# Weight loads and gathers that wait for one-element stores, and five operations of a token sort that run on VectorE

## The chip, the cores and the metric

One core of a Trainium2 chip runs the whole kernel. The metric is device time in microseconds (us) of one execution; each kernel is executed several times and the median counts. TensorE (PE) multiplies matrices, VectorE (DVE), ScalarE (ACT) and GpSimd (POOL) work on tiles, SyncE (SP) issues most of the DMAs, and POOL issues the indirect ones, the gathers and scatters by a list of row numbers.

## The reference

Three stages on 3072 tokens (4 sequences of 768) of width 384, all in float32:

```python
y = attn(r, k, v, w, u)            # linear attention with a decaying state, 8 heads of 48
e = argmax(x @ w_gate); g = softmax(x @ w_gate)[e]          # x: y, a row for each token
o = sigmoid(x @ w_output_gate)[e]
x = g * o * (relu(x @ w1[e]) @ w2[e])                       # one of 8 experts, 384 -> 1024 -> 384
out = (silu(x @ w_gate2) * (x @ w_val2)) @ w_out2           # 384 -> 1536 -> 384
```

## The kernel before

Each float32 product is made of three matmuls of rounded parts (high and low), so every weight and every activation is first split: ACT casts the high part, DVE subtracts it to get the low part.

**Order.** The attention stage, up to some 130 us, stands in an order written out by hand. The expert stage (130 to 370 us) and the last stage (370 us to the end) are put in order, engine by engine, by a scheduler when the program is built. On the chip each engine then runs its own list in that order, and an instruction waits for semaphores of the others. SP's list is one queue of DMA issues: an issue that waits holds up every later one.

**The expert stage.** Experts are taken by falling count of tokens, as positions e = 0 to 7, each with room for `CAPS[e]` tokens (416 to 360). For each position `run` goes through eight steps f, a step being 128 of the 1024 hidden columns: `step` multiplies w1 into PSUM (`ph`, two buffers), ACT and DVE make `h` out of it (L1207, L1208), and `second` multiplies w2 into `py` two steps later. Position 0 is done in two parts: its first 256 tokens inside the attention stage's pools (`head`, tiles `pha` and `pya`), the other 160 in `run`. So `run` begins with eight short steps (lines 1184 and 1185), and position 1 follows.

**Weights.** A group is two steps' worth of one expert: `r1` for w1 and `r2` for w2, 384 KB each, which `load` fetches into one of four raw buffers. Groups 0 to 3 are position 0's, 4 to 7 position 1's. `prefetch` splits a group (L1060 on ACT, L1063 on DVE) three groups ahead of its use, and then the raw buffer takes the group four further on. Before the first step, `run` issues groups 4 to 7 in one go.

**Tokens.** `gather` fetches a position's tokens by up to four indirect DMAs of 128 rows into `xg` (POOL, L1140), and `transposed` turns them on PE (`pt`, L1154) and splits them into `x` (L966, L967). There are two sets of these tiles, for even and for odd positions. The code asks for position e + 1 at step f = 3 of position e; the scheduler may put it earlier.

**Beside it**, `widen` turns the last stage's weights into float32 in 36 pieces, each with four DVE operations (L1025 to L1034) and one on POOL (L1031), and `sorted_positions` finds where each token goes, a few operations at a time between the steps: among them `t0` (L726), `dsel` (L741) and the four products of `dsel` (L744, L749; on DVE L746) with 576 elements in each partition.

Of the kernel before, what the change touches and what calls it, by code (L numbers as in the profile page):

```python
# [15 lines left out]
ALU = mybir.AluOpType  # L16
# [4 lines left out]
P = 128  # L21
# [7 lines left out]
CAPS = (416, 416, 412, 404, 392, 384, 372, 360)  # L29
# [9 lines left out]
def moe_kernel(ctx, tc, cst, small, tok, tr, u, w1, w2, m_gate, m_val, m_out, out):  # L39
    nc = tc.nc  # L40
    NT, DM = out.shape
# [3 lines left out]
    NTILE = NT // P  # L45
# [7 lines left out]
    NJ = -(-CAP // P)  # L53
# [12 lines left out]
    ident, mask, niota, rev8, slot, tile_i, part_i, lead, caps = (  # L66
        cs[:, at[n]] for n in ("ident", "mask", "niota", "rev", "slot", "tile", "part", "lead", "caps")
    )
# [9 lines left out]
    rows = const.tile([P, E * NJ], I32, name="rows")  # L78
# [196 lines left out]
    def ins(t, n, at):  # L275
        if at == 1:
            return t.rearrange("p (o e) -> p o e", o=1).to_broadcast([P, n, t.shape[1]])
        return t.rearrange("p (e o) -> p e o", o=1).to_broadcast([P, t.shape[1], n])
# [407 lines left out]
    def sorted_positions(pool, pool_ps):  # L686
# [36 lines left out]


        t0 = pool.tile([P, NTILE, E], F32, name="t0", bufs=1)
        nc.gpsimd.tensor_tensor(out=t0, in0=oh_all, in1=ins(off_f, NTILE, 1), op=ALU.mult)  # L726
        yield
        dpf = pool.tile([P, NTILE], F32, name="dpf")
        nc.vector.reduce_sum(dpf, t0, axis=AX.X)
# [11 lines left out]
        nc.vector.tensor_tensor(out=dsel, in0=ins(dhif, NTILE, 2), in1=ins(tile_i, NTILE, 1), op=ALU.is_equal)  # L741
        dsel2 = pool.tile([P, NTILE, 5, NTILE], BF16, name="dsel2", bufs=1)
        yield
        nc.gpsimd.tensor_tensor(out=dsel2[:, :, 0, :], in0=dsel, in1=ins(tile_i, NTILE, 2), op=ALU.mult)  # L744
        yield
        nc.vector.tensor_scalar(out=dsel2[:, :, 1, :], in0=dsel, scalar1=part_i, scalar2=None, op0=ALU.mult)  # L746
        for j in range(3):
            yield
            nc.gpsimd.tensor_tensor(out=dsel2[:, :, 2 + j, :], in0=dsel, in1=ins(scale3[:, j, :], NTILE, 2), op=ALU.mult)  # L749
        psd = pool_ps.tile([P, 5, NTILE], F32, name="psd", tag="pd")  # L750
        for i in range(0, NTILE, 4):
            doh = pool.tile([P, 4, P], BF16, name="doh", bufs=1)
# [218 lines left out]
class MoE:  # L971
# [67 lines left out]
                yield  # L1039
        nc.sync.dma_start(out=env["m32"][n - 1], in_=store)  # L1040

    def load(self, e, g):
        nc, env, GF = self.nc, self.env, 2
        if e and g == 0:
            self.ids[e] = bass.ds(nc.sync.value_load(env["ids"][0:1, e : e + 1], min_val=0, max_val=env["E"] - 1), 1)
        pe = self.ids[e]
        r1 = self.raw.tile([P, env["KD"], GF * P], F32, name="r1")
        nc.sync.dma_start(
            out=r1, in_=self.w1v[pe, :, :, g * GF * P : (g + 1) * GF * P].rearrange("o p k f -> (o p) k f")
        )  # L1050
        r2 = self.raw.tile([P, GF, env["DM"]], F32, name="r2")
        nc.sync.dma_start(out=r2, in_=self.w2v[pe, :, g * GF : (g + 1) * GF, :].rearrange("o p f d -> (o p) f d"))
        self.raws[e, g] = r1, r2

# [10 lines left out]
    def run(self, sorted_positions, gates, ffn):  # L1065
        nc, tc, env = self.nc, self.tc, self.env
        ident, x_d, rows, offs, yd = (env[x] for x in ("ident", "x_d", "rows", "offs", "yd"))
        CAP, NJ, KD, KF, DM, E, NT = (env[x] for x in ("CAP", "NJ", "KD", "KF", "DM", "E", "NT"))
        GF = 2
        c = self.c  # L1070
        early = ExitStack()
        self.cv = early.enter_context(tc.tile_pool(name="cv", bufs=2, reuse_waits="tile", side="right"))
        sp = early.enter_context(tc.tile_pool(name="sp", bufs=1, reuse_waits="tile", side="right"))
        self.xp.append(c.enter_context(tc.tile_pool(name="xp1", bufs=1, reuse_waits="tile")))
        p_y = c.enter_context(tc.tile_pool(name="p_y", bufs=1, space=PSUM, reuse_waits="tile"))
        p_h = c.enter_context(tc.tile_pool(name="p_h", bufs=2, space=PSUM, reuse_waits="tile"))
        p_t = c.enter_context(tc.tile_pool(name="p_t", bufs=2, space=PSUM, reuse_waits="tile"))
        p_d = c.enter_context(tc.tile_pool(name="p_d", bufs=1, space=PSUM, reuse_waits="tile"))

        NG = KF // GF  # L1080
        for n in range(len(PREFETCH), len(PREFETCH) + NG):
            self.load(*divmod(n, NG))

        def load_x(e, tiles):
            self.gather(e, tiles, rows[:, e * NJ + tiles[0] : (e + 1) * NJ], NT)
            return self.transposed(e, tiles, p_t, "pt")

        for _ in gates(sp):
            pass
        pos = sorted_positions(sp, p_d)  # L1090
        next(pos)
        for e in range(E):
            x, _ = self.xs.pop(e)
            sl = slice(0 if e else HEAD, CAPS[e])
            py = [p_y.tile([P, CAP], F32, name=f"py{d}") for d in range(KD)]
            for f in range(KF):
                if f % GF == 0:
                    wt = self.ahead.pop((e, f // GF))
                ph = p_h.tile([P, CAP], F32, name="ph")

                a, b = self.step(e, f, wt, x, sl, ph, py)
                with tc.issue_after(a), tc.issue_after(b):
                    if e == E - 1 and f == X_AT - 1:

                        nc.scalar.activation(ffn.warm, ffn.warm, AF.Sigmoid)
                    if e == E - 1 and X_AT <= f < X_AT + KD:
                        ffn.x_part(0, f - X_AT)
                    n = (e * KF + f) // GF + DIST
                    if len(PREFETCH) <= n < E * NG:
                        self.prefetch(*divmod(n, NG), f % GF)  # L1110
                        if f % GF == 1 and n + NG < E * NG:
                            self.load(*divmod(n + NG, NG))
                    if e * KF + f >= POS0 and f % POSK == 0:
                        next(pos, None)
                    if e * KF + f >= FILL0:
                        self.filler(FILLN)
                if (e, f) == (E - 1, 0):
                    for _ in pos:
                        pass
                    self.filler(1000)  # L1120
                    early.close()
                    self.first.close()
                    ffn.prepare()
                if f == 3 and e + 1 < E:
                    load_x(e + 1, range(-(-CAPS[e + 1] // P)))
        while self.pend:
            self.second()

    def gather(self, e, tiles, rows, last):

        nc, env = self.nc, self.env
        CAP, KD, DM = (env[x] for x in ("CAP", "KD", "DM"))
        pool = self.xp[e % 2]
        if tiles[0] == 0:
            x = pool.tile([P, 2, KD, CAP], F32R, name="x")
            self.xs[e] = x, pool.tile([P, env["NJ"], DM], F32, name="xg")
        xg = self.xs[e][1]
        for i, j in enumerate(tiles):
            n = min(P, CAPS[e] - j * P)
            nc.gpsimd.indirect_dma_start(  # L1140
                out=xg[0:n, j, :], out_offset=None, in_=env["x_d"][0:last, :],
                in_offset=bass.IndirectOffsetOnAxis(ap=rows[0:n, i : i + 1].bitcast(U32), axis=0),
            )
# [357 lines left out]
```

## Time and profile before

| what | value |
|---|---|
| median of 3 runs | 820.11 us (818.72 to 823.32) |
| the profiled execution | 828.89 us |
| its span, from the first to the last instruction | 827.1 us |
| mean granted clock of TensorE in it | 0.991 |
| PE busy | 790.2 us, 96% of the span |
| DVE, ACT, POOL busy | 515.1, 347.6, 210.6 us |

The profiled execution is one run with the hardware profiler on. Its rows are in us from the span's start. A row names the engine, the line of the kernel, the tiles written and read, and in brackets how long the engine had been idle before it and which instruction's end released it ("issue" where the profile shows nothing that it waited for). [...]

### The profile page before, as it was taken

To read this page: it belongs to the slowest core of one execution; us is meant where nothing else is said; L and a number is where in the kernel's file an instruction comes from. 1 tells how busy PE (TensorE), PEld (TensorE's weight loads), DVE (VectorE), ACT (ScalarE), POOL (GpSimd) and SP (SyncE) were. 2 spreads that over 40 slices of the span, in tenths; PEclk is the share of its full clock that TensorE was granted. 3 is DMA by queue.
4 is the path that set the end of the run, shared out by engine and by line. 5 is a ranking of instruction groups with operands and counts; after the bars stand their busy time and mean duration, and the time that the engine had idled before them with its cause. 6 is when DMAs were issued, how large, how long until landed. Compare 5 with 4: busy or idle time off the path is not lost.

```text
span 827.1 us, 15617 instructions
## 1 busy us (share of the span) xinstructions
PE 790.2 (96%) x5982; PEld 718.5 (87%) x5983; DVE 515.1 (62%) x1091; ACT 347.6 (42%) x791; POOL 210.6 (25%) x207
## 2 busy tenths in 40 slices
PE   7989779699999999999999999999999999999997
PEld 4877678688999999998888888888888888889997
DVE  7789997399999999955554335333533443344443
ACT  5878663364575576554432222212222222122322
POOL 6999951354524422200001000200020020001000
PEclk9999999899999999999999999999999999999999
DMA  8899933686777877342210000000000010001000
GB/s 322 297 361 334 332 128 108 215 268 194 253 222 260 252 245 253 89 139 86 86 59 32 19 1 13 39 0 1 14 39 1 0 45 1 1 7 40 1 20 24
DMA packets 61860, 99.28 MB, mean 120 GB/s; under 512 B 5461, under 2 KB 48105, under 8 KB 61776
## 3 DMA queue, kind: packets, MB, share of 16 engines
q1 hardware_dynamic: 58320, 88.34, 32.3%
q0 software_dynamic: 3456, 9.85, 3.5%
q8 instruction: 49, 0.80, 0.4%
q14 instruction: 35, 0.29, 0.1%
HBM read 81.64 MB, written 16.53 MB: 119 GB/s over the span
## 4 chain that ended last, share of the span: by engine, by line
issue 58%; PE 16%; DVE 4%; POOL 3%; DMA 1%; ACT 1%; POOLq 0%; SPq 0%; ACTq 0%; DVEq 0%
PE ph L1188 7%; PE py L1188 6%; POOL out_dram L1332 2%; PE pya L1188 1%; DMA m<-ab 1%; PE pha L1188 1%; DVE w2l L1063 1%; PE pt L1154 1%; DVE ab L1034 1%; DMA cva<-in_w_gate_dram 0%; DVE exw L1027 0%; PE ph L1184 0%; DVE ab L1030 0%; DVE h L1208 0%; DVE low L1033 0%
## 5 line engine op out<-in xcount | busy, mean ns | idle before, releaser
L1361 DVE TENSOR_TENSOR hv<-pg,hv 128x512 f32<-128x512 f32 (+1 forms) x84 | 51.6, 615 | 153.8 <-ACT hv L1360 153.7
L1332 POOL DMA_INDIRECT out_dram<-ot,tokd x24 | 24.8, 1035 | 448.3 <-DVE ot L1331 443.6
L1360 ACT ACTIVATE hv<-pg 128x512 f32<-128x512 f32 (+1 forms) x84 | 45.1, 537 | 167.4 <-PE pg L1356 167.2
L966 ACT CAST hh<-hv 128x512 fp32r<-128x512 f32 (+1 forms) x84 | 47.0, 560 | 142.1 <-DVE hv L1362 142.1
L1323 PE MATMUL po<-wh,hl 128*128 128x384 f32 x288 | 96.8, 337 | 0.0
L1323 PE MATMUL po<-wh,hh 128*128 128x384 f32 x288 | 96.8, 336 | 0.0
L1323 PE MATMUL po<-wl,hh 128*128 128x384 f32 x288 | 96.8, 336 | 0.0
L1356 PE MATMUL pg<-xh,wh 128*128 128x512 f32 (+1 forms) x252 | 91.2, 362 | 0.0
L1356 PE MATMUL pv<-xh,wl 128*128 128x512 f32 (+1 forms) x252 | 91.1, 362 | 0.0
L1356 PE MATMUL pg<-xh,wl 128*128 128x512 f32 (+1 forms) x252 | 91.1, 361 | 0.0
L1356 PE MATMUL pv<-xh,wh 128*128 128x512 f32 (+1 forms) x252 | 91.0, 361 | 0.0
L1356 PE MATMUL pv<-xl,wh 128*128 128x512 f32 (+1 forms) x252 | 91.0, 361 | 0.0
L1356 PE MATMUL pg<-xl,wh 128*128 128x512 f32 (+1 forms) x252 | 90.7, 360 | 0.0
L1188 PE MATMUL ph<-x,w1h 128*128 128x416 f32 (+6 forms) x336 | 88.3, 344 | 0.0
L967 DVE TENSOR_TENSOR hl<-hv,hh 128x512 fp32r<-128x512 f32 (+1 forms) x84 | 51.7, 616 | 45.8 <-ACT hh L966 45.6
L1362 DVE TENSOR_TENSOR hv<-pv,hv 128x512 f32<-128x512 f32 (+1 forms) x84 | 51.7, 615 | 45.1 <-PE pv L1356 43.6
L1188 PE MATMUL py<-h,w2h 128*128 128x416 f32 (+6 forms) x336 | 79.1, 340 | 0.0
L1031 POOL TENSOR_TENSOR low<-low,exw 128x384 f32<-128x384 f32 x36 | 42.5, 1180 | 114.9 <-DVE exw L1027 73.3
L482 ACT ACTIVATE dsb<-cs,cb 128x128 f32<-128x128 f32 x192 | 58.8, 389 | 25.0 <-DVE cb L478 25.0
L1188 PE MATMUL ph<-x,w1l 128*128 128x416 f32 (+6 forms) x168 | 59.8, 356 | 3.8 <-DVE h L1208 3.1
L1188 PEld LDWEIGHTS ph<-x,w1h 128*128 128x128 f32 x336 | 62.4, 191 | 0.2
L1188 PEld LDWEIGHTS py<-h,w2h 128*128 128x128 f32 x336 | 61.0, 188 | 0.1
(244 smaller groups left out, 1699.0 us busy)
## 6 DMA issues: line engine op xcount, KB each, us to landing
r<-in_w_dram SPq DMA_DIRECT2D x64, 384.0 KB, 4.5
yd_all<-in_tr_dram SPq DMA_DIRECT2D x24, 512.0 KB, 7.5
yd_all<-in_tok_dram SPq DMA_DIRECT2D x24, 384.0 KB, 5.3
m<-ab SPq DMA_DIRECT2D x36, 192.0 KB, 3.8
rw<-m SPq DMA_DIRECT2D x36, 192.0 KB, 2.4
yd_all<-in_tok_dram SPq DMA_DIRECT2D x24, 256.0 KB, 5.9
x_d<-xt SPq DMA_DIRECT2D x24, 192.0 KB, 5.5
cva<-in_w_gate_dram SPq DMA_DIRECT2D x12, 384.0 KB, 4.3
```

The costliest lines, as they stand in the source:

```text
L482: nc.scalar.mul(dsb[:, h, :], ident, cb[:, h : h + 1])
L966: first = nc.scalar.copy(hi, src)
L967: second = nc.vector.tensor_tensor(out=lo, in0=src, in1=hi.bitcast(F32), op=ALU.subtract)
L1031: nc.gpsimd.tensor_tensor(out=low, in0=low, in1=ex.bitcast(F32), op=ALU.mult)
L1034: nc.vector.scalar_tensor_tensor(out=bits, in0=pair[:, :, 1], scalar=-(2**31), in1=low.bitcast(I32), op0=ALU.bitwise_and, op1=ALU.bitwise_or)
L1188: nc.tensor.matmul(dst[:, 0:n], lhsT=a, rhs=b, start=start and t == 0, stop=stop and t == 2)
L1323: mm = nc.tensor.matmul(po[t], lhsT=a[:, t * P : (t + 1) * P], rhs=bb, start=(f == 0 and j == 0), stop=(f == KF2 - 1 and j == 2))
L1332: st = nc.gpsimd.indirect_dma_start(out=out[:, :], out_offset=bass.IndirectOffsetOnAxis(ap=tokd[:, i : i + 1].bitcast(U32), axis=0), in_=o ...
L1356: nc.tensor.matmul(dst, lhsT=a[:, fs], rhs=bb[:, q, :], start=(q == 0 and j == 0), stop=(q == KD - 1 and j == 2))
L1360: nc.scalar.activation(hv, pg, AF.Sigmoid)
L1361: nc.vector.tensor_tensor(out=hv, in0=pg, in1=hv, op=ALU.mult)
L1362: nc.vector.tensor_tensor(out=hv, in0=pv, in1=hv, op=ALU.mult)
```

## The change

Three things. Of the four groups that `run` loaded at its beginning, groups 6 and 7 are now asked for after steps 0 and 2 of position 0, and each of their two loads first waits for DVE to store one zero into the buffer that it fills. Position 2's gathers, which the scheduler was free to put early, wait for a store of DVE into `xg` that comes after step 0 of position 1; the transposes of that position stay where they were in the code. And `t0` and the four products of `dsel` that POOL made are made by DVE.

```diff
-        nc.gpsimd.tensor_tensor(out=t0, in0=oh_all, in1=ins(off_f, NTILE, 1), op=ALU.mult)
+        nc.vector.tensor_tensor(out=t0, in0=oh_all, in1=ins(off_f, NTILE, 1), op=ALU.mult)
...
-        nc.gpsimd.tensor_tensor(out=dsel2[:, :, 0, :], in0=dsel, in1=ins(tile_i, NTILE, 2), op=ALU.mult)
+        nc.vector.tensor_tensor(out=dsel2[:, :, 0, :], in0=dsel, in1=ins(tile_i, NTILE, 2), op=ALU.mult)
...
         for j in range(3):
             yield
-            nc.gpsimd.tensor_tensor(out=dsel2[:, :, 2 + j, :], in0=dsel, in1=ins(scale3[:, j, :], NTILE, 2), op=ALU.mult)
+            nc.vector.tensor_tensor(out=dsel2[:, :, 2 + j, :], in0=dsel, in1=ins(scale3[:, j, :], NTILE, 2), op=ALU.mult)
...
-    def load(self, e, g):
+    def load(self, e, g, gate=None):
...
         r1 = self.raw.tile([P, env["KD"], GF * P], F32, name="r1")
+        if gate:
+            gate.memset(r1[0:1, 0, 0:1], 0.0)
         nc.sync.dma_start(
...
         r2 = self.raw.tile([P, GF, env["DM"]], F32, name="r2")
+        if gate:
+            gate.memset(r2[0:1, 0, 0:1], 0.0)
...
-        for n in range(len(PREFETCH), len(PREFETCH) + NG):
+        for n in range(len(PREFETCH), len(PREFETCH) + 2):
             self.load(*divmod(n, NG))
...
-        def load_x(e, tiles):
-            self.gather(e, tiles, rows[:, e * NJ + tiles[0] : (e + 1) * NJ], NT)
-            return self.transposed(e, tiles, p_t, "pt")
+        def gathered(e, gate=None):
+            self.gather(e, range(-(-CAPS[e] // P)), rows[:, e * NJ : (e + 1) * NJ], NT, gate)
...
+                    if e == 0 and f in (0, 2):
+                        self.load(*divmod(len(PREFETCH) + 2 + f // 2, NG), nc.vector)
+                    if (e, f) == (1, 0):
+                        gathered(2, nc.vector)
...
                 if f == 3 and e + 1 < E:
-                    load_x(e + 1, range(-(-CAPS[e + 1] // P)))
+                    if e != 1:
+                        gathered(e + 1)
+                    self.transposed(e + 1, range(-(-CAPS[e + 1] // P)), p_t, "pt")
...
-    def gather(self, e, tiles, rows, last):
+    def gather(self, e, tiles, rows, last, gate=None):
...
         xg = self.xs[e][1]
+        if gate:
+            gate.memset(xg[0:1, tiles[0] : tiles[-1] + 1, 0:1], 0.0)
```

What this does to the engines' lists shows at three places. First SP's list where `run` begins (`r_2775` is group 5's w1, `r_2779` and `r_2781` are group 6, `r_2783` and `r_2785` group 7; the loads of the position's number, L1045, follow). Before:

```order
L1048 DMA r_2775<-in_w_dram 128x3x256
L1052 ISA
L1052 DMA r_2777<-in_w_dram 128x2x384
L1048 ISA
L1048 DMA r_2779<-in_w_dram 128x3x256
L1052 ISA
L1052 DMA r_2781<-in_w_dram 128x2x384
L1048 ISA
L1048 DMA r_2783<-in_w_dram 128x3x256
L1052 ISA
L1052 DMA r_2785<-in_w_dram 128x2x384
L1045 TENSOR_LOAD ids
```

And of the change (`r_2838` and `r_2841` are group 6 now, `r_2876` and `r_2879` group 7, `r_2928` group 8's w1; the lines of the changed kernel are 11 further on below the diff's last part):

```order
L1050 DMA r_2775<-in_w_dram 128x3x256
L1056 ISA
L1056 DMA r_2777<-in_w_dram 128x2x384
L1045 TENSOR_LOAD ids
...
L1050 DMA r_2838<-in_w_dram 128x3x256
L1056 ISA
L1056 DMA r_2841<-in_w_dram 128x2x384
L1050 ISA
L1050 DMA r_2876<-in_w_dram 128x3x256
L1056 ISA
L1056 DMA r_2879<-in_w_dram 128x2x384
L1050 ISA
L1050 DMA r_2928<-in_w_dram 128x3x256
```

Groups 6 and 7 went behind the loads of the positions' numbers, and group 8 and all that follows stands behind their waits.

Second POOL's list from position 1's gathers (the rows of 128 and of 32 tokens) to the products of `dsel`; 28, 20 and 8 tokens are the last gathers of positions 2, 3 and 4. Before:

```order
L1140 DMA xg<-x_d,rows 128x384 x3
L1140 DMA xg<-x_d,rows 32x384
L726 TENSOR_TENSOR t_3214<-oh_all,off_f 128x192
L1140 DMA xg<-x_d,rows 128x384 x3
L1140 DMA xg<-x_d,rows 28x384
L1031 TENSOR_TENSOR low<-low,exw 128x384
L1140 DMA xg<-x_d,rows 128x384 x3
L1140 DMA xg<-x_d,rows 20x384
...
L1031 TENSOR_TENSOR low<-low,exw 128x384 x5
L744 TENSOR_TENSOR dsel_3345<-dsel,cs 128x24x24
L749 TENSOR_TENSOR dsel_3345<-dsel,scale_66 128x24x24 x3
```

And of the change:

```order
L1151 DMA xg<-x_d,rows 128x384 x3
L1151 DMA xg<-x_d,rows 32x384
L1151 DMA xg<-x_d,rows 128x384 x3
L1151 DMA xg<-x_d,rows 20x384
L1031 TENSOR_TENSOR low<-low,exw 128x384 x3
L1151 DMA xg<-x_d,rows 128x384 x3
L1151 DMA xg<-x_d,rows 28x384
L1031 TENSOR_TENSOR low<-low,exw 128x384 x2
```

Position 3's gathers moved ahead of position 2's, and those came behind three of the 36 products of `widen`; `t0` and `dsel` are gone from this list.

Third DVE's list around the first product of `dsel`. Before:

```order
L741 TENSOR_TENSOR dsel<-dhif,cs 128x576
L1025 TENSOR_SCALAR ab<-ab 128x384
L1033 TENSOR_TENSOR low<-ab,low 128x384
L1208 SCALAR_TENSOR_TENSOR h<-ph,h 128x416
L1034 SCALAR_TENSOR_TENSOR ab<-cva,low 128x384
L1063 TENSOR_TENSOR w1l<-r_3089,w1h 128x768
L1027 TENSOR_SCALAR exw<-ab 128x384
L1034 SCALAR_TENSOR_TENSOR ab<-cva,low 128x384
L1208 SCALAR_TENSOR_TENSOR h<-ph,h 128x416
```

And of the change, from the same operation:

```order
L741 TENSOR_TENSOR dsel<-dhif,cs 128x576
L1030 TENSOR_SCALAR ab<-ab 128x384
L1067 TENSOR_TENSOR w1l<-r_3093,w1h 128x768
L744 TENSOR_TENSOR dsel_3350<-dsel,cs 128x24x24
L1033 TENSOR_TENSOR low<-ab,low 128x384
L1027 TENSOR_SCALAR exw<-ab 128x384
L1219 SCALAR_TENSOR_TENSOR h<-ph,h 128x416
```

One product stands in this step; the other three stand one each in steps 4, 6 and 8 from there.

## Rows read from the trace of the kernel before

**Rows 1.** Stretches of 20 us: length, busy time of PE, PEld, DVE, ACT, POOL, granted clock, DMA share, GB/s.

```profile
200.00:220.00 20.00, 16.90 (x82) 15.76 (x81) 20.00 (x33) 11.83 (x25) 13.98 (x10) 0.91 0.67 195
...
240.00:260.00 20.00, 20.00 (x119) 19.02 (x118) 19.83 (x37) 12.98 (x25) 8.28 (x7) 1.00 0.73 232
```

**Rows 2.** Timeline of PE (TensorE matmuls), 156 to 166 us: start, duration, line, tiles, [idle before <-releaser].

```profile
156.44 0.63 PE L1184 MATMUL ph<-x,w1h 128*128 128x320 f32 x1 [6.43 <-issue]
...
159.41 0.84 PE L1154 MATMUL pt<-cs,xg 128*128 128x128 f32 x3
...
163.50 0.35 PE L1184 MATMUL ph<-x,w1h 128*128 128x320 f32 x1
...
165.05 0.35 PE L1184 MATMUL py<-h,w2h 128*128 128x320 f32 x1
```

**Rows 3.** Timeline of ACT (ScalarE).

```profile
156.02 0.37 ACT L1232 COPY yd_all<-pya 128x256 f32<-128x256 f32 x1 [2.48 <-remote]
...
172.58 0.84 ACT L1060 CAST w1h<-r 128x768 fp32r<-128x768 f32 x1
```

**Rows 4.** Timeline of SP's queue: the first and the last of eight weight loads.

```profile
145.72 0.40 SPq L1048 DMA_DIRECT2D r<-in_w_dram  x1
...
151.57 0.04 SPq L1052 DMA_DIRECT2D r<-in_w_dram  x1
```

**Rows 5.** Timeline of POOL (GpSimd).

```profile
145.95 0.96 POOL L1140 DMA_INDIRECT xg<-x_d,rows  x1 [3.14 <-DVE scale L273]
...
155.12 0.91 POOL L1140 DMA_INDIRECT xg<-x_d,rows  x1 [0.30 <-issue]
...
201.04 1.68 POOL L744 TENSOR_TENSOR dsel<-dsel,cs 128x576 bf16<-128x576 f32 x1 [2.46 <-DVE dsel L741]
202.68 4.51 POOL L749 TENSOR_TENSOR dsel<-dsel,scale 128x576 bf16<-128x576 f32 x3
...
218.86 1.02 POOL L1031 TENSOR_TENSOR low<-low,exw 128x384 f32<-128x384 f32 x1
```

**Rows 6.** DMA between 147 and 160 us.

```profile
DMA packets 3115, 4.40 MB, mean 338 GB/s; under 512 B 256, under 2 KB 2797, under 8 KB 3115
```

**Rows 7.** Two stretches at half clock, columns as in Rows 1.

```profile
153.40:160.20 6.80, 3.75 (x16) 3.76 (x17) 0.55 (x2) 1.70 (x6) 2.02 (x3) 0.50 0.95 348
...
208.03:211.45 3.42, 3.29 (x10) 3.19 (x11) 3.42 (x8) 1.73 (x4) 0.44 (x1) 0.50 0.69 203
```

**Rows 8.** Timeline of PE, 202 to 212 us.

```profile
202.25 0.46 PE L1188 MATMUL ph<-x,w1l 128*128 128x412 f32 x1 [0.84 <-DVE h L1208]
...
208.16 0.71 PE L1188 MATMUL ph<-x,w1l 128*128 128x412 f32 x1 [2.26 <-DVE h L1208]
...
211.42 1.34 PE L1188 MATMUL py<-h,w2h 128*128 128x416 f32 x6
```

**Rows 9.** Timeline of DVE (VectorE).

```profile
193.25 0.55 DVE L1034 SCALAR_TENSOR_TENSOR ab<-cva,low 128x384 int32<-128x384 int32 x1
193.72 0.95 DVE L1063 TENSOR_TENSOR w1l<-r,w1h 128x768 fp32r<-128x768 f32 x1
...
195.69 0.35 DVE L1027 TENSOR_SCALAR exw<-ab 128x384 int32<-128x384 int32 x1
...
200.21 0.75 DVE L741 TENSOR_TENSOR dsel<-dhif,cs 128x576 f32<-128x576 f32 x1
...
203.06 1.90 DVE L1063 TENSOR_TENSOR w1l<-r,w1h 128x768 fp32r<-128x768 f32 x1
204.88 1.31 DVE L1027 TENSOR_SCALAR exw<-ab 128x384 int32<-128x384 int32 x1
206.11 1.50 DVE L1034 SCALAR_TENSOR_TENSOR ab<-cva,low 128x384 int32<-128x384 int32 x1
...
218.52 2.19 DVE L1063 TENSOR_TENSOR w1l<-r,w1h 128x768 fp32r<-128x768 f32 x1
```

**Rows 10.** Timeline of DVE at the start of the kernel.

```profile
0.99 0.06 DVE L376 MEMSET yd_all<- 128x4 f32 x1
```

## The prediction

> **What bounds the kernel now.** I began with the table of 20 us stretches. What the reader is to see there is that TensorE has no room in most of the run: it is busy for 20.00 of 20.00 us from 240 us on, with VectorE at 19.83, while between 200 and 220 us it is busy for 16.90, with VectorE at 20.00 [rows 1]. A gain can only come from the places where TensorE waits, and from 150 to 220 us, where the change works, there are two of them. TensorE's timeline gives both.
>
> **Stall 1** ends at 156.44 us, where the first short step of `run` begins after 6.43 us of idle time that the profile puts down to nothing [rows 2]. Just ahead of it ACT is late with the copies that empty `pya`: the one at 156.02 us stood 2.48 us for a semaphore of another engine, though TensorE had stopped at 150.0 (156.44 less 6.43) [rows 2, 3]. In the same stretch SP issues eight weight loads (groups 4 to 7, 8 x 384 KB = 3.1 MB) [rows 4] and POOL eight gathers, those of positions 1 and 2 [rows 5], and the DMA engines move 4.40 MB from 147 to 160 us, at 338 GB/s [rows 6]. [...] The twelve matmuls of the first short step take 2.97 us (156.44 to 159.41); the same twelve of a later step take 1.55 (163.50 to 165.05) [rows 2]. So stall 1 costs 6.43 + 1.42 = 7.85 us in this execution.
>
> **Stall 2** ends at 208.16 us. TensorE stands 0.84 and then 2.26 us for `h` of VectorE, and behind the second wait the clock is 0.50 again: the nine matmuls from 208.16 to 211.42 take 3.26 us [rows 7, 8], half of which, 1.63, full clock would save. Together 0.84 + 2.26 + 1.63 = 4.73 us. VectorE's timeline shows why `h` is late: while POOL makes the four products of `dsel` (201.04 to 207.19, 202.68 + 4.51) [rows 5], VectorE's operations stretch. L1063 takes 1.90 us where it took 0.95 some 9 us earlier, L1027 1.31 for 0.35, L1034 1.50 for 0.55 [rows 9], an excess of 0.95 + 0.96 + 0.95 = 2.86 us.
>
> **Part 1, the two gates.** Removed from the crowd are groups 6 and 7 (4 x 384 KB = 1.57 MB) and position 2's gathers, 412 rows of 1,536 bytes (0.63 MB). Those 2.2 MB are, at 338 GB/s [rows 6], 6.5 us of transfer; what is left (4.40 - 2.2) would be done by about 153.5 us. In a profiled execution stall 1 should then shrink by at least the 156.4 - 153.5 = 2.9 us that the crowd ends earlier and at most by all of its 7.85.
>
> How much of that the median gets is the main unknown. The profiled execution took 828.89 us and the median of the plain runs is 820.11: the one is 8.78 longer, and stall 1 is the only place with a pause of that size that no work explains. [...] The bounds for term 1 are 0 and 7.85 us; I take 1.0, near the lower end, since 7.85 and 8.78 are so close; something is left because the same 4.40 MB go through the same queues without a profiler. [...]
>
> What the gates add. Group 6 is asked for after step 0, whose w1 part begins at 156.44 us; its first reader on ACT comes at 172.58 [rows 2, 3]. A load of 2 x 384 KB at 338 GB/s takes 2.3 us, so some 13 us of cover are left, and the same for group 7, two steps later and read later. On SP's queue group 8 and what follows stand behind these waits; they wait for free raw buffers anyway, and would be late only if the cover of group 6 were gone, at about 2.3 us for each group. Position 2's gathers now stand behind step 0 of position 1, and behind position 3's on POOL. Their transposes come only after step f = 3; 0.63 MB is 1.9 us of transfer and four issues of some 0.95 us [rows 5], 5.7 us in all, against about four steps of 3 to 6 us each (208.16 less 202.25 is one). So I cost the gates' delay at nothing; without that cover it would be up to 5.7 us. Position 3's gathers wait for position 1's transposes instead, with a whole position to spare. The five stores cost VectorE what its smallest memset shows, 0.06 us [rows 10], 0.3 in all.
>
> **Part 2, the five operations.** VectorE gets four products of 576 elements; L741, of that size and before POOL had begun, took 0.75 us [rows 9]: 4 x 0.75 = 3.0. `t0` has 192 elements in a partition, a third, 0.25. That is 3.25 us added against 2.86 taken away with POOL's products: VectorE's own account comes out at +0.4, or +0.7 with the stores. But the four no longer stand in one place: one goes into each of the steps at which the order shows them, so that each step's `h` is late by 0.75 at most, not by 2.86 at once. If the steps between have slack, TensorE's whole 4.73 goes; if VectorE is the bound through all of 200 to 220 us, where it is busy for 20.00 of 20.00 [rows 1], nothing goes but the slow clock may. Bounds 0 and 4.73; I take the middle, 2.4. It cannot lie near the upper end, since the row with 20.00 leaves VectorE no idle time to put them in; nor near zero, since three of the four leave the stretch.
>
> **Sum.** Against the median: 820.11 - 1.0 - 2.4 + 0.3 = 817.0 us. Against the profiled execution's own 828.89: - 5.4 (the middle of 2.9 and 7.85) - 2.4 + 0.3 = 821.4, that is, in a profile more of the gain shows than in the median.
>
> **Rivals.** *Stall 1 is real in plain runs.* Then the median gains what the profile shows: 820.11 - (2.9 to 7.85) - 2.4 + 0.3, 810.2 to 815.1. For it: a saturated stretch, at a place where eight loads and eight gathers meet. Against it: the 8.78 us between profile and median would then have no place in the trace.
>
> *Nothing is gained.* Stall 1 is the profiler's, and VectorE gives back all that it got: 820.11 + 0.4 + 0.3 = 820.8, with a gain or loss of some 1.5 around it. For it: VectorE is the bound of its stretch [rows 1].
>
> *VectorE becomes the bound: slower.* POOL still makes L1031, 1.02 us each, and beside one of them at 218.86 us L1063 took 2.19 where it takes 0.95 [rows 5, 9]. If each moved product meets one of these and stretches by the same 1.24, they cost 3.0 + 4 x 1.24 + 0.25 = 8.2 against 2.86: VectorE is 5.4 us later. Stall 2 remains, and with the stores the time is 820.11 + 5.4 + 0.3 = 825.8. This decides from the point where each of the four meets a whole L1031; with one met only, the time is 822.1. [...] Against this rival: without the four products (6.15 us to the end of the last) POOL is busy for at most 13.98 - 6.2 = 7.8 of the 20 us [rows 1, 5], gathers included, so that a product has at most 4 chances in 10 to meet anything there.
>
> **How the numbers follow.** About 0.42 for the forecast, 814.5 to 819.5 by itself (term 1 from 0 to 3, term 2 from 0.9 to 4.7); 0.30 for the first rival, about 808 to 814.5; 0.18 for no gain, 819.5 to 822.5; 0.10 for the slower rival, 822.5 to 826.5. The range takes the forecast, nearly all of the first rival and no gain: 809.5 to 822.5, which leaves out 0.10 above and some 0.05 to 0.1 below. A difference under 0.5% (4.1 us) is about what a measurement of this kernel can't tell from none: faster is below 816.0, which is the first rival and a third of the forecast, 0.30 + 0.15 = 0.45; slower is above 824.2, most of the slower rival, 0.08; the rest, 0.47, is the same.
>
> **What would show it.** In the changed profile: DMA between 147 and 160 us at about 2.2 MB less; SP's group 6 issued after the first short step; TensorE's idle time before that step below 3.5 us; a profiled time closer to the median than 8.78. L1063 near 0.95 us where the four products were, each product at about 0.75, no 2.26 us wait for `h`, no half clock behind it. The prediction is wrong if TensorE waits for casts of group 6 or 7 or for position 2's transposes, if the products take 1.5 us or more, or if the median gains over 4 us while the profiled excess over it stays.

## The result, and the profile after

The change takes 826.31 us (median of 14 runs, 823.95 to 828.36), the kernel before 820.95 in the same comparison (14 runs, 818.72 to 823.32): 1.0063 times as long, 95% interval 1.0051 to 1.0075. So it is slower by 5.4 us, where 3 us of gain were forecast.

The profiled execution of the change, though, took 825.88 us, 3.0 less than the one of before (828.89), with a span of 824.1 against 827.1. The trace shows what was gained and what was lost. First TensorE's timeline where `run` begins (start, duration, line, tiles, idle time and what ended it):

```profile
150.14 0.42 PE L1195 MATMUL ph<-x,w1h 128*128 128x320 f32 x1 [0.15 <-ACT yd_all L1243]
```

The first short step comes at 150.14 us instead of 156.44 [rows 2], after 0.15 us of idle time instead of 6.43. Stall 1 is gone from this profile. What comes behind it got longer: from the first short step to the first matmul of the last stage (`pg`) it is 366.69 - 150.14 = 216.55 us, and 370.19 - 156.44 = 213.75 before, which still has the half clock behind stall 1 in it (0.50 from 153.40 to 160.20 us [rows 7], 1.42 us by the prediction's reading); without it the part behind the start is 4.2 us longer. The stretches of the change, below the one of before that the rows do not have (length, busy time of PE, PEld, DVE, ACT, POOL, granted clock as a share of full speed, DMA share, GB/s):

```profile
160.00:180.00 20.00, 19.08 (x134) 18.06 (x133) 18.66 (x44) 16.98 (x43) 10.37 (x11) 0.99 0.61 180
```

```profile
140.00:160.00 20.00, 19.55 (x158) 18.74 (x157) 14.31 (x63) 10.68 (x31) 6.74 (x7) 1.00 0.67 220
160.00:180.00 20.00, 17.07 (x83) 15.79 (x83) 17.38 (x40) 11.91 (x26) 13.74 (x12) 0.83 0.77 256
170.00:177.10 7.10, 6.35 (x19) 5.89 (x20) 7.10 (x17) 3.56 (x9) 5.14 (x4) 0.52 0.88 293
200.00:220.00 20.00, 18.02 (x101) 17.22 (x101) 17.84 (x33) 9.59 (x20) 8.00 (x7) 1.00 0.75 221
...
240.00:260.00 20.00, 18.57 (x107) 17.67 (x106) 17.46 (x33) 11.43 (x23) 7.61 (x6) 1.00 0.78 246
```

TensorE is idle for 2.93 us between 160 and 180, where it was idle for 0.92, and from 170 to 177 its granted clock is 0.52. Between 200 and 220, where it had 3.10 us of idle time [rows 1], it has 1.98 now, and between 240 and 260, where it had none, 1.43. From the first short step to the last stage TensorE is busy for 208.60 of the 213.75 us before and for 208.79 of the 216.55 after: 2.6 us more of idle time, and some 1.4 us more of half clock (about half of the 6.35 us here, half of the 3.29 at stall 2), make up nearly all of the 4.2. TensorE's timeline gives the waits:

```profile
163.84 0.45 PE L1199 MATMUL ph<-x,w1l 128*128 128x416 f32 x1 [0.69 <-DVE hs L1216]
...
168.06 0.42 PE L1195 MATMUL py<-h,w2h 128*128 128x320 f32 x1 [0.55 <-DVE h L1219]
...
170.37 0.63 PE L1195 MATMUL py<-h,w2h 128*128 128x320 f32 x1 [1.31 <-DVE h L1219]
```

```profile
208.50 0.46 PE L1199 MATMUL py<-h,w2l 128*128 128x412 f32 x1 [1.98 <-ACT yd_all L1243]
```

```profile
249.80 0.45 PE L1199 MATMUL ph<-x,w1l 128*128 128x404 f32 x1 [1.25 <-DVE h L1219]
```

The first ones are VectorE's doing. Its timeline, and POOL's beside it:

```profile
163.47 0.54 DVE L1216 TENSOR_TENSOR hs<-hs,ph 128x160 f32<-128x160 f32 x2
166.40 1.36 DVE L1033 TENSOR_TENSOR low<-ab,low 128x384 f32<-128x384 f32 x1 [2.39 <-POOL low L1031]
```

```profile
149.68 0.87 POOL L1151 DMA_INDIRECT xg<-x_d,rows  x1 [0.30 <-issue]
159.40 0.96 POOL L1151 DMA_INDIRECT xg<-x_d,rows  x1 [8.85 <-DVE hs L1216]
...
164.41 0.90 POOL L1151 DMA_INDIRECT xg<-x_d,rows  x1 [0.31 <-issue]
165.34 2.00 POOL L1031 TENSOR_TENSOR low<-low,exw 128x384 f32<-128x384 f32 x2
```

POOL stands 8.85 us with the first of position 3's gathers, which needs the tile that position 1's transposes still read, then issues four of them in 5.9 us, and only then makes the first two L1031. VectorE has come to L1033, which wants the first of these, and stands 2.39 us, with the next `h` queued behind it. That is the move that the order showed on POOL's list, position 3's gathers ahead of the products of `widen`.

The wait at 208.50 us is ACT's. Its timeline and SP's queue:

```profile
206.67 0.54 ACT L1021 ACTIVATE low<-cva 128x384 f32<-128x384 uint32 x1 [4.04 <-DMA cva<-in_w_out_dram]
207.12 0.49 ACT L1218 ACTIVATE h<-ph 128x412 fp32r<-128x412 f32 x1
```

```profile
152.90 0.38 SPq L1050 DMA_DIRECT2D r<-in_w_dram  x1
...
201.70 0.35 SPq L1005 DMA_DIRECT2D cva<-in_w_out_dram  x1
```

The load of the ninth piece of `widen` (L1005) was issued at 201.70 us and ACT started on it 5.0 us later; ACT stood 4.04 us for it with the next `h` behind, and TensorE waited for ACT. The first of the two SP rows is group 6, asked for after the first short step, as forecast.

The moved products, on VectorE's timeline, against 0.75 us for the row that priced them [rows 9]:

```profile
196.23 1.58 DVE L744 TENSOR_TENSOR dsel<-dsel,cs 128x576 bf16<-128x576 f32 x1
...
213.66 0.74 DVE L749 TENSOR_TENSOR dsel<-dsel,scale 128x576 bf16<-128x576 f32 x1
...
222.35 0.75 DVE L749 TENSOR_TENSOR dsel<-dsel,scale 128x576 bf16<-128x576 f32 x1
...
229.51 1.35 DVE L749 TENSOR_TENSOR dsel<-dsel,scale 128x576 bf16<-128x576 f32 x1
```

### The profile page after: what moved, and what is told of

It is laid out like the page before. It is cut to its first block, busy times and chain, and to the rows that moved or that the text cites. A ratio compares the mean times of both kernels' runs of the same rounds, so it can differ in the third digit from the quotient of the medians.

```text
span 824.1 us, 15614 instructions
## 1 busy us (share of the span) xinstructions
PE 790.6 (96%) x5982; PEld 717.9 (87%) x5983; DVE 511.6 (62%) x1101; ACT 347.5 (42%) x791; POOL 206.0 (25%) x202
## 4 chain that ended last, share of the span: by engine, by line
issue 57%; PE 13%; DVE 5%; DMA 4%; POOL 3%; ACT 1%; POOLq 0%; SPq 0%; ACTq 0%; DVEq 0%
PE ph L1199 6%; PE py L1199 5%; POOL out_dram L1343 2%; DMA m<-ab 2%; DMA r<-in_w_dram 1%; DMA xg<-x_d,rows 1%; DVE w1l L1067 1%; DVE low L1033 1%; PE pha L1199 1%; DVE h L1219 1%; DVE ab L1034 1%; DMA cva<-in_w_out_dram 1%; DVE w2l L1067 1%; PE pya L1199 1%; PE pt L1165 0%
## 5 line engine op out<-in xcount | busy, mean ns | idle before, releaser
L1031 POOL TENSOR_TENSOR low<-low,exw 128x384 f32<-128x384 f32 x36 | 42.3, 1180 | 101.5 <-DVE exw L1027 82.4
```

The lines of the kernel that those rows point to most:

```text
L1031: nc.gpsimd.tensor_tensor(out=low, in0=low, in1=ex.bitcast(F32), op=ALU.mult)
```

## The experiments

Each was compared with runs of the kernel before on the same chip, in five groups on four chips. There the kernel before took 829.74 (e1 to e4), 828.49 (e5 to e8), 828.79 (e9 to e12), 829.88 (e13 to e16) and 828.39 us (e17 and e18), not 820.95; what that does to the verdicts is the first thing that they show. "Ahead" is TensorE's idle time ahead of the first step of `run` in the profile of each.

| run | edit | us | ratio to before, 95% | ahead, us |
|---|---|---|---|---|
| e4 | before, unchanged | 829.40 (one) | | 6.48 |
| e5 | the change | 828.32 | 0.9996 (0.9984 to 1.0008) | 2.42 |
| e16 | the change | 827.96 | 0.9974 (0.9958 to 0.9989) | 2.45 |
| e2 | five operations on DVE alone | 830.47 | 1.0006 (0.9990 to 1.0023) | 7.90 |
| e1 | both gates alone | 827.37 | 0.9973 (0.9957 to 0.9989) | 2.47 |
| e6 | group gates alone | 830.00 | 1.0018 (1.0007 to 1.0028) | 5.23 |
| e10 | gather gate alone | 827.47 | 0.9989 (0.9970 to 1.0008) | 2.44 |
| e12 | the change without group gates | 824.80 | 0.9964 (0.9948 to 0.9981) | 2.41 |
| e3 | the change, position 3 gated too | 827.86 | 0.9982 (0.9963 to 1.0001) | 2.48 |
| e7 | same, position 2's gate earlier | 825.55 | 0.9960 (0.9944 to 0.9976) | 2.41 |
| e15 | no group gates, all gathers gated | 828.15 | 0.9979 (0.9964 to 0.9995) | 2.45 |
| e8 | the change, L1031 of pieces 0 to 2 on DVE | 823.71 | 0.9936 (0.9923 to 0.9950) | 2.41 |
| e9 | before, same edit | 830.82 | 1.0029 (1.0015 to 1.0042) | 6.38 |
| e11 | both gates alone, same edit | 827.63 | 0.9997 (0.9982 to 1.0011) | 2.44 |
| e13 | the change, pieces 5 and 6 on DVE | 825.58 | 0.9942 (0.9922 to 0.9962) | 2.44 |
| e14 | before, same edit | 831.91 | 1.0026 (1.0008 to 1.0045) | 6.43 |
| e17 | the change, pieces 0, 1, 5, 6 on DVE | 823.68 | 0.9934 (0.9909 to 0.9958) | 2.42 |
| e18 | e12 and pieces 0 to 2 on DVE | 823.71 | 0.9934 (0.9910 to 0.9959) | 2.44 |

**Is stall 1 in plain runs?** The kernel before and the change, unchanged, once more.

> The kernel before, unchanged, for a second profiled execution. If the 6.43 us of idle PE at 150 to 156.4 us come with every profiled execution, the span is near 827 again and the stall stands at the same place. If they were an accident of that one execution, PE's first short step begins near 150.2 us and the span is near 819.

> The change itself, timed beside the runs of this job. In the first four runs the kernel before took 829.7 us where the comparison that gave the result had 820.95, and its profile shows the stall of 6.4 us ahead of run again. Theory S (that stall is in plain runs on some chips and not on others): where before takes about 829.7 us, this kernel takes 825 to 828 and is the faster one; where before takes about 821, it takes 826 and is the slower one. Theory T (the time of all kernels differs between chips by a factor): this kernel is slower by 0.6% here too, about 834.7 beside 829.7.

> The change once more, as the level for the runs beside it. If the stall ahead of run is there in the runs of before (about 829 us), the change is within 0.3% of before, as on the other chip; if before takes about 821, the change takes 826.

TensorE's timeline of the kernel before, again, and of the change:

```profile
156.46 0.64 PE L1184 MATMUL ph<-x,w1h 128*128 128x320 f32 x1 [6.48 <-issue]
```

```profile
151.14 0.41 PE L1195 MATMUL ph<-x,w1h 128*128 128x320 f32 x1 [2.42 <-ACT yd_all L1243]
```

The profiled execution took 829.40 us and the 28 runs of before beside it 829.74: here plain runs are as long as the profiled one, so the profiler does not make the stall. By its price (6.48 and 1.4 of half clock, 7.9) these runs stand above the 820.95 of the comparison that gave the result (8.8, 7.5, 7.8, 8.9 and 7.4). So, by their times, the runs of before in the comparison of the result had no stall 1, and those on the four chips here had it, all of them; the profile of before that the prediction read was of the second kind. The change has 2.4 us of it left where the result's profile had 0.15, and takes 828.3 and 828.0 instead of 826.3. Theory S gave 825 to 828 and a change that is the faster one; 828.32 and 827.96 are at the end of that range, and only the second is faster clear of noise. T, which asked for about 834.7, fell. That it is the chip itself, and nothing else about that comparison, is not shown. Where stall 1 exists, the change is as fast as before or 0.26% faster; where it does not, the change has nothing to remove and shows only what it costs. The rest asks what that is.

**Which part costs?**

```diff
-        nc.gpsimd.tensor_tensor(out=t0, in0=oh_all, in1=ins(off_f, NTILE, 1), op=ALU.mult)
+        nc.vector.tensor_tensor(out=t0, in0=oh_all, in1=ins(off_f, NTILE, 1), op=ALU.mult)
```

(with the four products of `dsel`, forward on the kernel before for e2, and taken back from the change for e1; e6 and e10 are e1 without the gather's and without the groups' gate, e12 is the change without the groups' gate)

> The kernel before with only the five operations of the sort moved to VectorE, no gate. Theory A: no gather is in L1031's way, so the loss of the gates is absent, and the products on VectorE cost about as much as they free: 817 to 821.5 us. Theory B: the whole loss is here, 824 to 828. Theory C: no gate, 817 to 821.5.

> The change with its five operations of the sort back on POOL: only the gates are left. Theory A (the gates let POOL's list put position 3's gathers ahead of the first L1031, POOL waits with them until position 1's transposes are done at 159.4 us, and L1033 on VectorE, then PE, wait for L1031; price about 2.9 us of idle PE and 3.3 of half clock): this kernel has the same order, so it is slow too, 823 to 828 us. Theory B (the loss is VectorE's extra 3.25 us of products): no loss is left, 817 to 821 us. Theory C (the gates make SP's later loads late, ACT waits for them): slow as in A, 823 to 828.

> The kernel before with only the gates of groups 6 and 7. Position 2's gathers are early again, but on POOL's list position 3's still stand ahead of the first L1031. Theory A (POOL's list is what costs): the wait of L1033 for L1031 is there as with the whole change, 2 us or more, and the time is 826 to 829 us where before takes 829.7. Theory A2 (position 2's gathers, late through their gate, are what costs): no loss after the first short step, 822 to 825 us.

> The kernel before with only position 2's gathers held by the store. One L1031 stands ahead of position 3's gathers here, the later ones behind them. Theory A: about half of the loss after the first step, so less slow there than with both gates. For the stall ahead of run: if the indirect gathers make it (four of eight leave the stretch), PE's idle time falls from 6.4 us to near the 2.4 us that it has with both gates, and the time is 824 to 827 where before takes about 829; if the weight loads make it, it stays above 5 us and the time is 828 to 831.

> The change without the gates of groups 6 and 7. One L1031 stands ahead of position 3's gathers. Theory A: VectorE waits less for POOL than with the whole change, so 1 to 4 us below it, if the stall ahead of run does not grow by more than the 1.2 us that the group gates alone took off it: 825 to 828 where before takes about 829. Rival: the group gates carry the gain ahead of run, and the time is 829 to 831.

The five operations alone change nothing (+0.7 us, the interval holds 0). TensorE's timeline of e2 at the place of stall 2:

```profile
204.47 0.46 PE L1188 MATMUL ph<-x,w1l 128*128 128x412 f32 x1 [1.12 <-DVE h L1208]
...
214.76 0.45 PE L1188 MATMUL py<-h,w2l 128*128 128x412 f32 x1 [0.97 <-ACT yd_all L1232]
```

Instead of 0.84 and 2.26 us [rows 8] it stands 1.12 and 0.97, 1.0 us less; but ahead of `run` it stands 7.90 where e4 has 6.48. Why that stall is longer here is not shown. Theory B, that these products are the loss, falls with e2.

The stall ahead of `run`, with the group gates alone and with the gather gate alone:

```profile
154.16 0.64 PE L1192 MATMUL ph<-x,w1h 128*128 128x320 f32 x1 [5.23 <-issue]
```

```profile
151.77 0.64 PE L1193 MATMUL ph<-x,w1h 128*128 128x320 f32 x1 [2.44 <-ACT yd_all L1241]
```

Four gathers less take off 4.0 us, with or without the group gates (2.44 in e10, 2.47 in e1); the 1.57 MB of groups 6 and 7 take off 1.2 alone and nothing beside the gather gate.

The loss behind that point is estimated as a part's difference to before, plus the idle time that it saved ahead of `run`: e1 -2.4 + 4.0 = 1.6 us, e6 1.5 + 1.2 = 2.8, e10 -1.3 + 4.0 = 2.7, e12 -4.0 + 4.1 = 0.1, the change -0.2 + 4.1 = 3.9 (e5) and -1.9 + 4.0 = 2.1 (e16), in the comparison of the result 5.4. So each gate alone costs some 2.7 us behind the start, both 1.6, and the products nothing, but the parts do not add up: gather gate and products together cost nothing, and with the group gates on top 2 to 5.4. These sums are rough: each carries an interval of 0.9 to 1.6 us either way and the idle time of one profile, and they leave out the half clock behind the stall. The mean granted clock from 140 to 160 us is 0.84 in the profile of before and 0.83 in those of e1, e6 and e10, but 1.00 in those of e12 and e16; 0.83 is 6.8 us at 0.50, so part of the difference between e12 and e10 is this. Clear of that are e6's 2.8 us and the loss of the change in e5 and in the comparison of the result; how the rest divides is not.

Against the expectations: those of e1 and e2 were written for the level of 820.95 and are read here as differences. e6 took 830.00, above the ranges of both of its theories. e10 took the branch of the gathers, 2.44 us, and 827.47 against its 824 to 827. e12 at 824.80 is just below A's 825 to 828, and its rival falls. With e1, stall 2 is still there, beside POOL's products as before: from 200.15 to 205.63 us POOL makes the four, and L1027 on VectorE, 0.35 us at 198.01, takes 1.42 at 200.14. TensorE's timeline:

```profile
208.44 0.46 PE L1199 MATMUL ph<-x,w1l 128*128 128x412 f32 x1 [1.64 <-DVE h L1219]
...
212.18 0.45 PE L1199 MATMUL ph<-x,w1l 128*128 128x412 f32 x1 [0.41 <-DVE h L1219]
```

**Is it POOL's list near 165 us?**

```diff
-                    if (e, f) == (1, 0):
-                        gathered(2, nc.vector)
+                    if (e, f) in ((1, 0), (2, 0)):
+                        gathered(e + 1, nc.vector)
```

(e3; in e7 position 2's stands at `(0, 4)`; in e15 all stand at step 6, two positions ahead)

> The change with one more gate: position 3's gathers too are held by a store of VectorE, after step 0 of position 2, so that POOL reaches L1031 without waiting behind them. Theory A: PE's idle time at 163 to 173 us and the half clock behind it (2.9 + 3.3 us) are gone, 826.3 - (4 to 6) = 820 to 822 us. Theory B: nothing changes, 825 to 828. Theory C: nothing changes, 825 to 828.

> The change, with the store for position 2's gathers after step 4 of position 0 and one more for position 3's after step 0 of position 2: on POOL's list the first L1031 stands behind position 1's gathers alone, and position 2's gathers are not late. Theory A: no wait of L1033 for L1031, no wait of PE for a gather, 3 to 5 us below the change, 821 to 824 us where the change takes 826. Theory D (VectorE's work from 160 to 270 us is the bound, so that a wait removed in one place comes back in another): 825 to 828.

> The five operations on VectorE, no gates of weight groups, and every gather from position 2 on held by a store of VectorE that stands after step 6 two positions ahead: no gather stands on POOL in front of a product that is ready while it waits for PE. Theories A1 and C2 both: PE's idle time from 160 to 260 us below 4 us, 821 to 825 us where before takes about 829. Theory D (VectorE's work is the bound whatever POOL does): no better than the run without group gates, 825 to 828.

VectorE's timeline of e3 has no wait at the first L1033 any more, but TensorE's has waits a little later, the second for the gather of position 2 itself:

```profile
161.84 0.55 DVE L1033 TENSOR_TENSOR low<-ab,low 128x384 f32<-128x384 f32 x1
```

```profile
172.34 0.45 PE L1199 MATMUL ph<-x,w1l 128*128 128x416 f32 x1 [1.38 <-DVE xg L1148]
...
178.14 0.55 PE L1165 MATMUL pt<-cs,xg 128*128 128x128 f32 x3 [1.96 <-DMA xg<-x_d,rows]
```

The wait was removed as A said and the time did not follow (827.86, where A gave 820 to 822 on the level of 826.3, about 822 to 824 on this one). e7 gains 2.8 us on the change beside it, less than A's 3 to 5; e15 gains nothing. A wait of POOL's list was exchanged for a wait for late gathers (1.96 us in e3, 3.12 in e7, 4.02 in e15). The stretch from 160 to 180 us of e3, and of e12, where no L1033 waits for POOL there either:

```profile
160.00:180.00 20.00, 15.60 (x92) 14.17 (x93) 20.00 (x45) 12.92 (x29) 8.50 (x8) 1.00 0.85 256
```

```profile
160.00:180.00 20.00, 16.75 (x98) 15.06 (x97) 20.00 (x43) 13.14 (x30) 14.19 (x12) 1.00 0.80 254
```

TensorE is idle for 4.40 and 3.25 us, more than the 2.89 of the change in e5 and e16, with VectorE busy all the time. So theory A alone does not carry the loss. D's case, waits that come back elsewhere, fits e3 and e15; but e15 did not meet its own condition, TensorE's idle time from 160 to 260 being 6.4 us and not below 4.

**L1031 off POOL.**

```diff
-            nc.gpsimd.tensor_tensor(out=low, in0=low, in1=ex.bitcast(F32), op=ALU.mult)
+            (nc.vector if i < 3 else nc.gpsimd).tensor_tensor(out=low, in0=low, in1=ex.bitcast(F32), op=ALU.mult)
```

(e8 on the change, e9 on the kernel before, e11 on both gates alone; `i in (5, 6)` in e13 and e14, `(0, 1, 5, 6)` in e17; e18 is e8 without the group gates)

> The change, with the first three of the 36 products of L1031 on VectorE instead of POOL (about 0.55 us each): nobody waits for POOL while its list stands behind position 3's gathers. Theory A: the 2.4 us wait of VectorE and most of the 6 us behind it are gone, for 1.7 us more work: 822 to 824.5 us where the change takes 826. Theory D: no gain, 826 to 829.

> Control for the run that put the first three products of L1031 on VectorE: the same edit on the kernel before, without any gate. Theory A (that run gained because POOL's list held L1031 back behind position 3's gathers, as the change has it): here nothing is held back for long, so no gain; 1.7 us more work on VectorE, 0 to 2 us slower than before. Rival E (VectorE does these products faster, whatever POOL's list): the same gain of 4 to 5 us as there.

> Both gates, the sort's five operations on POOL as before, and the first three products of L1031 on VectorE. Theory A: the wait for POOL is gone here too, some 3 to 5 us below the gates alone (which were 0.27% below before): about 0.7% below before, 822 to 824.5 us where before takes about 829. If the moved operations of the sort are neutral, it equals the change with L1031 on VectorE.

e8 is 4.6 us faster than the change beside it (e5), although VectorE makes three L1031 more (0.54, 0.55 and 0.55 us); the same edit costs 2.0 us on the kernel before and gains nothing on the gates alone. By the ratios of the change (0.9996 in e5, 0.9974 in e16) e8 gains 3 to 5 us. So the gain belongs to the change as a whole, and rival E falls; but e11 missed what A gave it, and in its profile TensorE waits 3.43 us for ACT near 211 us. Where e8 gains is seen in the stretches of e5 and of e8:

```profile
160.00:180.00 20.00, 17.11 (x102) 15.73 (x101) 18.51 (x44) 12.89 (x30) 12.76 (x11) 1.00 0.84 268
200.00:220.00 20.00, 16.72 (x83) 15.47 (x82) 17.55 (x33) 9.91 (x21) 7.48 (x6) 0.91 0.71 206
```

```profile
160.00:180.00 20.00, 16.61 (x102) 15.12 (x101) 19.39 (x48) 13.83 (x32) 9.88 (x9) 1.00 0.93 293
200.00:220.00 20.00, 19.11 (x105) 18.11 (x104) 19.55 (x37) 10.17 (x21) 9.22 (x7) 1.00 0.77 240
```

Between 160 and 180, where A looked for it, TensorE is busy for less in e8, 16.61 us against 17.11. Most of the gain is between 200 and 220: 19.11 against 16.72, at full clock. That is the place of ACT's wait for the ninth piece. The next runs are for that place.

> The change, with L1031 of pieces 5 and 6 alone on VectorE: up to position 2's gathers POOL's list is that of the change, but L1034 of piece 5 no longer waits behind position 4's gathers. Theory C2 (the loss is the wait near 208 us: POOL behind position 4's gathers, then L1034, then the load, then ACT with h behind it): ACT's 4 us wait and PE's 2 to 3 us of idle time with half clock behind it are gone, 3 to 5 us below the change. Theory A1 (the loss is the wait near 165 us): no gain, within 1 us of the change.

> The same edit on the kernel before, the control. Theory C2: no such wait there, so 0 to 2 us slower than before, as with the first three pieces. If it gains 3 us or more here too, VectorE simply makes these products better and C2 is not shown by the other run.

ACT's timeline there, of the change (e16) and of e13:

```profile
207.80 0.54 ACT L1021 ACTIVATE low<-cva 128x384 f32<-128x384 uint32 x1 [3.80 <-DMA cva<-in_w_out_dram]
208.25 0.50 ACT L1218 ACTIVATE h<-ph 128x412 fp32r<-128x412 f32 x1
```

```profile
201.84 0.56 ACT L1021 ACTIVATE low<-cva 128x384 f32<-128x384 uint32 x1 [1.51 <-DVE ab L1034]
202.29 0.50 ACT L1218 ACTIVATE h<-ph 128x412 fp32r<-128x412 f32 x1
...
206.35 0.51 ACT L1218 ACTIVATE h<-ph 128x412 fp32r<-128x412 f32 x1
```

and the stretches of both:

```profile
200.00:220.00 20.00, 17.22 (x79) 15.86 (x78) 18.08 (x34) 9.51 (x20) 7.50 (x6) 0.83 0.76 223
220.00:240.00 20.00, 20.00 (x114) 19.45 (x113) 20.00 (x37) 12.35 (x24) 5.22 (x5) 1.00 0.70 219
```

```profile
200.00:220.00 20.00, 20.00 (x111) 19.42 (x111) 18.42 (x36) 9.73 (x21) 12.99 (x6) 1.00 0.74 232
220.00:240.00 20.00, 17.73 (x93) 15.28 (x93) 19.22 (x36) 10.63 (x21) 5.93 (x5) 1.00 0.67 196
```

In e13 `h` stands ahead of the load's reader on ACT's list, nobody waits 3.80 us, and TensorE is busy for 20.00 us from 200 to 220 instead of 17.22, at a granted clock of 1.00 instead of 0.83. Of these gains 2.3 us are lost again between 220 and 240. By the medians 2.4 us are left (825.58 against 827.96 beside it), less than the 3 to 5 expected; the control loses 2.0. But the profiled execution of e13 is the slowest of its five (828.37, against 827.23 for e16's), so these two profiles show one wait exchanged for others and not where the 2.4 us come from. One link held in part only: SP issued that load at 201.83 in e13 and at 203.07 in e16, 1.2 us earlier, less than the 3.80; most of the wait went away through ACT's order, not through an earlier L1034.

> The change with L1031 of pieces 0, 1, 5 and 6 on VectorE. If the waits near 165 and near 208 us are two costs, their gains add up less 1.1 us of work: 5 to 7 us below the change, about 0.8% below before. If it is one cost met twice, or VectorE's own work is the bound by then, it is no better than with pieces 0 to 2 alone: 0.5 to 0.65% below before.

> The change without the group gates and with L1031 of pieces 0 to 2 on VectorE. If the group gates cost something of their own beside POOL's list, this is 1 to 3 us better than the change with the same edit: 0.75 to 1% below before. If they cost only through that list, the two are equal, about 0.65% below before. If the order that the scheduler finds by accident is what matters, it can come out worse, 0.2 to 0.4% below.

The gains do not add up: e17 and e18 stand where e8 stood, 0.65% below before, which is the second branch that was given for each. Two edits that meet the change at different places end at the same 823.7 us. Where stall 1 is present, this version beats both kernels (0.9936, 0.9934 and 0.9934). In the conditions of the result, where the change took 826.31, it wasn't measured; taking e8's 4.6 us off gives some 821.7 there, level with before. That is an estimate.

## Why the prediction was wrong

- **Stall 1 and its price.** The 7.85 us are right where it exists, and the choice of near nothing for the median (term 1, 1.0 us) was right too, by luck, since its reason was wrong: I read the 8.78 us between profile and median as the profiler's work. The runs showed plain executions that by their times have the stall; e4, profiled, is within 0.4 us of the plain ones beside it (829.40 and 829.74), which speaks against that reading. No run shows the 1.0 us of term 1: what the runs showed in its place is 4.0 us less idle time ahead of `run` on those chips (6.48 in e4, 2.42 and 2.45 in e5 and e16) and, in the comparison of the result, by the times, no stall to shorten. The first rival, that plain runs have the stall, was true, by the times, on four chips, and even there the change gained 0.04 to 0.26%, since the loss behind it took the rest.
- **What crowds that stretch.** I counted bytes, 2.2 MB less. The DMA of the changed kernel in that window:

```profile
DMA packets 3236, 4.11 MB, mean 317 GB/s; under 512 B 197, under 2 KB 3076, under 8 KB 3236
```

 That is 0.29 MB less than before [rows 6] and not 2.2, since groups 6 and 7 are still issued within it (152.90 to 155.53 us) and group 8's w1 at 156.14 instead of 164.14. This profile has no stall, but by its times the kernel before has none in that comparison either, so the experiments decide: the 0.63 MB of four gathers took off 4.0 us, the 1.57 MB of two groups 1.2. From 148 to 160 us, summed from the rates of stretches of 2 us, e10 moves 3.28 MB and stands 2.44 us, e6 only 2.26 MB and stands 5.23. In these profiles the stall goes with the gathers and not with the bytes.
- **The step that failed** is the one that cost the gates' delay at nothing, with "position 3's gathers wait for position 1's transposes instead, with a whole position to spare". I asked when the gathers' readers come, and not who stands behind them on POOL's list: L1031, behind it L1033 on VectorE, behind that `h`. The runs showed the gates at 1.6 to 2.8 us behind the start, by those rough sums, where nothing was forecast (clear of noise for the group gates alone, 2.8), and the whole change at 5.4 in the comparison of the result. The trace shows the chain through POOL's list (2.39 us of VectorE); that it carries this cost is not shown, since in e3 and e12 it is gone and TensorE is idle there for longer. ACT's wait for the ninth piece is the second place that the forecast had at nothing.
- **Term 2** was mis-sized: 2.4 us of gain forecast, 0.7 of loss measured by itself (interval -0.8 to 1.9). VectorE's account was right in kind: four products took 1.58, 0.74, 0.75 and 1.35 us, 4.4 against 3.0; two of them met an L1031 of POOL, and one of these passed the 1.5 us that the prediction had named as a sign of being wrong. TensorE's 2.26 us for `h` did go, as forecast; in the change a 1.98 us wait for ACT took the place, which the prediction did not see.
- **The slower rival** gave 825.8 us, close to the 826.3, but by a mechanism that the trace bears out in part only: it needed four products that meet an L1031, two did, and e2 shows that they cost nothing in the end. The chance of 0.08 for slower was too small, because waits that an order can bring were priced at nothing wherever I saw cover.
- **What held:** group 6 issued after the first short step, no wait for groups 6 and 7, TensorE's idle time there below 3.5 us (0.15, and 2.42 and 2.45 in e5 and e16), a profiled time close to the median (825.88 and 826.31), no half clock near 208 us in that profile.

What stays open: how the 5.4 us divide in the conditions of the result. In its profile the waits are 2.93 us near 163 to 172 with a granted clock of 0.52 behind, 1.98 near 208 and 1.25 near 250, against 1.69 (four waits, 170 to 181 us), 3.10 and none before; in e5 and e16, the same program, the lower clock fell near 210 instead (0.57 and 0.58 from 210 to 214 us in e5, 0.50 to 0.58 from 210 to 216 in e16). No run in those conditions took these apart, so which wait carries the loss stays open. Nor is it shown what makes the stall ahead of `run` come and go. The loading of code is not seen in it: in the profile of before no packet of an instruction queue is among the 3,115 packets of the DMA from 147 to 160 us.

## What to carry to other kernels

Before a transfer is made to wait, read the list of the engine that issues it and ask what stands behind the waiting instruction, two engines further on too; the cover of the transfer's own reader says nothing of them (here VectorE stood 2.39 us for an L1031 behind four gathers). Where a scheduler orders the lists, an edit can order them anew and the parts need not add up (e8, e17 and e18 all ended at 823.7 us), so measure each part alone and together. A wait that an edit removes from a profile is not yet time (in e3 the 2.39 us went, and it takes 0.9982 of before, the change 0.9996 and 0.9974): see whether the time follows. And when a profile and the plain times of one kernel differ by the price of one stall, run it again, profiled and plain in one go, before the difference is put down to anything.

## What the runs showed of the hardware

- The same program, the kernel before, took 820.95 us in the comparison of the result and 828.39 to 829.88 in the five others, 7.4 to 8.9 us more, about the price of one stall (7.9). TensorE's idle time there: 6.4 to 7.9 us in the five profiles that had eight gathers and all the loads ahead of `run`, 5.23 in the one with eight gathers and fewer loads, 2.41 to 2.48 in all thirteen with four gathers, 0.15 in the one of the result, with four as well.
- Not every wait takes TensorE's clock down: in e3 waits of 1.38 and 1.96 us at 172 and 178 us passed at a granted clock of 1.00 from 160 to 180 us, while in the change 0.55 and 1.31 us at 168 and 170 were followed by 0.52 over 7.1 us.
